# Turning one tile in eight of u with TensorE instead of VectorE's blocks, in a one-core spectral MoE kernel

## The chip, the core and the metric

The program runs on one core of one Trainium2 chip. The metric is the device time of one execution in microseconds. One execution of each program was also recorded by the hardware profiler; its span runs from the first to the last instruction of the program and is a little shorter than the device time. Engines are named as in the profile: PE (TensorE matmul), PEld (its weight loads), DVE (VectorE), ACT (ScalarE), POOL (GpSimd) and SP (SyncE, which issues most transfers here).

## What is computed

Three stages follow each other: a spectral mixing layer (Fourier transform along the sequence, complex matrix, soft threshold, inverse transform), a soft mixture of experts, and a SoLU layer with layer norm. The change lies in the last one:

```python
def _moe2_ref(x, w_in, w_out, g_ln):
    h = x @ w_in
    h_max = np.max(h, axis=-1, keepdims=True)
    e = np.exp(h - h_max)
    sm = e / (np.sum(e, axis=-1, keepdims=True) + 1e-09)
    solu = h * sm
    mu = np.mean(solu, axis=-1, keepdims=True)
    var = np.mean((solu - mu) ** 2, axis=-1, keepdims=True)
    ln = (solu - mu) / np.sqrt(var + 1e-06) * g_ln
    return (ln @ w_out).astype(np.float32)
```

Here x has 24576 rows of 256, w_in is 256 x 1024 and w_out 1024 x 256. All of it is wanted in fp32 precision.

## The kernel before, in words

`phase1` does the spectral layer and the sums of the mixture for eight batches. `phase2` does the experts, and then the SoLU layer in a loop over `NI` = 192 tiles of 128 rows. Only that loop changes, so only it is told here.

The mixture's output is never stored: it has rank 32 per batch, and `gst` holds the slots' outputs already multiplied by w_in, split into a high and a low part on the partitions, while `ctt` holds the combine weights. So `hmat(i)` makes h of tile i with two matmuls of 512 columns into `hps`, a PSUM tile of two banks from a pool of three. With the sign turned, `rowmax(i)` (DVE, line 996) reduces h, `expo(i)` (ACT, line 1003) takes the exponential and its row sum, and `umul(i)` (DVE, line 1011) forms u = h times e with its row sum. `vari(i)` (ACT, line 1087) sums the squares for the variance. The mean and g are folded into the weights `gw` beforehand, and the row's scale is applied when the result leaves PSUM.

For the last product u must be transposed, in eight blocks of 128 columns. `blocks(i)` has DVE transpose u in 32 x 32 squares (line 1027, tile `tb`) and then issues four transfers on SP (line 1031), which move the squares between partitions into `t2`. `tb` and `t2` have three buffers each. `uhi(i)` rounds t2 to fp32r, six blocks on ACT (line 1067) and two on POOL (line 1068), and `ulo(i, n)` forms the rest, t2 minus its rounded part, on POOL in two halves (line 1077). `prod(i)` is then 24 matmuls of 256 columns in fp32r: high part times high weights and times low weights (16), low part times high weights (8). Tiles come in pairs in one PSUM bank (`po2`, two buffers): the product of an even tile has to wait until both outputs of the pair four tiles earlier have been copied out by `outp` (ACT, line 1129). `rstd` makes the scales of four tiles at a time on POOL (lines 1112 to 1115). The last two tiles (`direct`) are turned by PE (`trans`, `direct_parts`) with `gstn`, a copy of `gst` in the natural order of columns, since `blocks` wants its columns permuted.

The order is written by hand: every engine runs its instructions in the order in which the loop at the end of `phase2` writes them. In turn i of the loop PE gets `hmat(i + 3)` and `prod(i - 3)`; DVE `rowmax(i + 2)`, `umul(i + 1)`, `blocks(i + 1)`; ACT `outp(i - 6)`, `vari(i)`, `expo(i + 2)`, `uhi(i - 1)`; POOL its share of `uhi(i - 1)`, `ulo(i - 1)` and `rstd(i)`. SP also gets the stores of the output (line 1140, every fourth turn) and the loads of `ct` (line 861, four transfers every eighth turn). In turns 24 to 30 `last_c` adds eight operations on POOL (lines 1153 and 1154), and in turn 40 `gst_order` adds one (line 1019). A tile of u has four buffers, `uh` and `ul` have four each.

Of the kernel before, what the change touches and what calls it, by code (L numbers as in the profile page):

```python
# [35 lines left out]
def kernel(  # L36
# [808 lines left out]
    def phase2(p2: ExitStack, pw: ExitStack):  # L845
# [3 lines left out]
        gw = k_p.tile([128, 8, 2, D], F32R, name="gw")  # L849
        gw_h, gw_l = gw[:, :, 0, :], gw[:, :, 1, :]  # L850
        gst = k_p.tile([128, DFF], F32R, name="gst")
        gstn = k_p.tile([128, DFF], F32R, name="gstn")
        cts = {}


# [96 lines left out]
        def right(name, bufs, **k):  # L952
            return p2.enter_context(tc.tile_pool(name=name, bufs=bufs, side="right", **k))

        e_p = right("e_p", 2)
        u_p = right("u_p", 4)
        o_p = right("o_p", 2)
# [19 lines left out]
        def hmat(i):  # L977
            if i >= NI:
                return
            j, k = divmod(i, 4)  # L980
            ps = ph_p.tile([128, DFF], F32, name="hps", tag="hps")
            for fh in range(2):
                mm(ps[:, 512 * fh:512 * fh + 512], ctt[j][:, 128 * k:128 * k + 128], (gstn if direct(i) else gst)[:, 512 * fh:512 * fh + 512])
            hps[i] = ps

        def stats(i):
# [19 lines left out]
        def umul(i):  # L1006
            if i >= NI:
                return
            st, k = stats(i)
            u = u_p.tile([128, DFF], F32, name="u", tag="u")  # L1010
            DVE.scalar_tensor_tensor(out=u, in0=hps.pop(i), scalar=1.0, in1=et.pop(i), op0=ALU.mult, op1=ALU.mult, accum_out=st[:, 2, k:k + 1])  # L1011
            ut[i] = u


        def direct(i):
            return i >= NI - 2

        def gst_order():
            POOL.tensor_copy(out=gstn.rearrange("p (c j b) -> p b c j", c=8, b=4), in_=gst.rearrange("p (b c j) -> p b c j", b=4, c=8).bitcast(F32))

        def blocks(i):
            if i >= NI or direct(i):
                return
            t = u_p.tile([128, DFF], F32, name="tb", tag="tb", bufs=3)
            DVE.transpose(out=t, in_=ut[i])  # L1027
            t2 = u_p.tile([128, 4, 256], F32, name="t2", tag="t2", bufs=3)
            for a in range(4):
                z = slice(32 * a, 32 * a + 32)  # L1030
                SP.dma_start(out=t2[:, a, :], in_=t[z].rearrange("i (b x) -> i b x", b=4))  # L1031
            t2t[i] = t2
# [23 lines left out]
                DVE.tensor_tensor(out=ul[:, z, :], in0=ps[:, z, :], in1=uh[:, z, :].bitcast(F32), op=ALU.subtract)  # L1056


        HA = 6

        def uhi(i):
            if i < 0 or direct(i):
                return
            uh, ul = parts(i)
            v = t2t[i].rearrange("p a (c j) -> p c a j", c=8)
            w = uh.rearrange("p c (a j) -> p c a j", a=4)
            ACT.activation(out=w[:, 0:HA], in_=v[:, 0:HA], func=AF.Copy)  # L1067
            POOL.tensor_copy(out=w[:, HA:8], in_=v[:, HA:8])  # L1068

        def ulo(i, n):  # L1070
            if i < 0 or direct(i):
                return
            uh, ul = uht[i]
            z = slice(4 * n, 4 * n + 4)
            v = t2t[i].rearrange("p a (c j) -> p c a j", c=8)[:, z]
            w = uh[:, z, :].rearrange("p c (a j) -> p c a j", a=4)
            POOL.tensor_tensor(out=ul[:, z, :].rearrange("p c (a j) -> p c a j", a=4), in0=v, in1=w.bitcast(F32), op=ALU.subtract)  # L1077
            if n:
                t2t.pop(i)
# [6 lines left out]
            sq = e_p.tile([128, DFF], F32, name="sq", tag="sq", bufs=1)  # L1086
            ACT.activation(out=sq, in_=ut.pop(i), func=AF.Square, bias=st[:, 2, k:k + 1], scale=-float(DFF), accum_out=st[:, 3, k:k + 1])  # L1087

        def prod(i):
            if i < 0 or i >= NI:  # L1090
                return
            uh, ul = uht.pop(i)
            if i % 2 == 0:
                pot[i // 2, 0] = po_p.tile([128, 2, D], F32, name="po2", tag="po2")
            ps = pot[i // 2, 0][:, i % 2, :]
            for f in range(8):
                mm(ps, uh[:, f, :], gw[:, f, 0, :], f == 0, False)
                mm(ps, uh[:, f, :], gw[:, f, 1, :], False, False)
            for f in range(8):
                mm(ps, ul[:, f, :], gw[:, f, 0, :], False, f == 7)  # L1100
            pot[i] = ps


        def rstd(i):
# [9 lines left out]
            POOL.tensor_tensor(out=st[:, 3, k], in0=st[:, 3, k], in1=st[:, 1, k], op=ALU.add)  # L1114
            POOL.tensor_tensor(out=st[:, 4, k], in0=st[:, 3, k], in1=mhalf[:, k], op=ALU.pow)

        o_todo = {}

        def outp(i):
            if i < 0:  # L1120
# [55 lines left out]
        blocks(0)  # L1176
        for i in range(NI + 6):
            j, k = divmod(i, 4)
            hmat(i + 3)
            trans(i)  # L1180
            rowmax(i + 2)
            umul(i + 1)
            blocks(i + 1)
            store(i - 6)
            late_c(i)
            last_c(i)
            outp(i - 6)
            vari(i)
            expo(i + 2)
            direct_parts(i)  # L1190
            if i <= NI:
                uhi(i - 1)
                ulo(i - 1, 0)
            rstd(i)
            if i <= NI:
                ulo(i - 1, 1)
            if i == 40:
                gst_order()
            if k == 1:
                pieces(j + 2)  # L1200
            prod(i - 3)
        while o_todo:
            store(min(o_todo))

# [139 lines left out]
```

## Time and profile before

| | us |
|---|---|
| device time, three runs | 1366.03, 1366.82 (median), 1371.24 |
| span of the profiled execution | 1364.4 |
| the loop over 192 tiles, first u (654.31) to the end of the span | 710 |
| DVE busy in the span | 1207.1 (88%) |
| PE busy in the span | 1268.9 (93%) |

The profiled execution's own device time is not listed apart; its span lies 2.4 us below the median of the runs and 1.6 us below the fastest, which is what lies around the first and the last instruction. A share of the whole span says little here, since the program has stages with different limits; the loop is read by itself. Starts within the span are read as they stand in the timeline, in us from the span's start.

### The profile page before, as it was taken

How to read it: one execution, taken by the hardware profiler on the slowest of the kernel's cores; microseconds unless marked ns; L12 is line 12 of the kernel's file. 1: busy time of each engine (PE TensorE's matmuls, PEld its weight loads, DVE VectorE, ACT ScalarE, POOL GpSimd, SP SyncE). 2: the span in 40 equal slices, each digit the busy share in tenths (PEclk: the TensorE clock that was granted, in tenths of full speed). 3: DMA queues.
4: the chain of work that ended last, by engine and by line, in shares of the span. 5: the costliest groups of instructions: out<-in, count | busy, mean ns of one | idle time of the engine just before them, and what ended most of it. 6: DMA issues, size and time to landing. Idle time of an engine off the chain costs nothing.

```text
span 1364.4 us, 30891 instructions
## 1 busy us (share of the span) xinstructions
PE 1268.9 (93%) x10784; PEld 1126.9 (83%) x10784; DVE 1207.1 (88%) x1691; ACT 1038.8 (76%) x2005; POOL 979.4 (72%) x1045
## 2 busy tenths in 40 slices
PE   6999999999999999878699989999999999899998
PEld 3888888888878788855588888988898889888897
DVE  7787988888888989765999999999999999999994
ACT  5567665666667665533799889999899999899995
POOL 5557575757565654221588989989899999889996
PEclk8899999999999999999799999999999999999999
DMA  8966463646445464168478788778877888787874
GB/s 267 289 202 175 124 193 111 209 117 186 140 144 167 126 181 155 62 223 291 108 179 220 188 210 209 198 197 209 205 194 203 196 198 217 196 206 191 201 197 125
DMA packets 190746, 252.70 MB, mean 185 GB/s; under 512 B 21504, under 2 KB 155392, under 8 KB 190592
## 3 DMA queue, kind: packets, MB, share of 16 engines
q1 hardware_dynamic: 190256, 249.57, 67.3%
q8 instruction: 85, 1.39, 0.4%
q10 hardware_dynamic: 336, 1.18, 0.2%
q14 instruction: 69, 0.57, 0.1%
HBM read 91.94 MB, written 59.11 MB: 111 GB/s over the span
## 4 chain that ended last, share of the span: by engine, by line
PE 37%; POOL 14%; DMA 13%; issue 12%; DVE 10%; SPq 8%; ACT 6%; POOLq 0%; ACTq 0%; DVEq 0%
PE po L89 10%; DMA t<-tb 9%; POOL ul L1077 8%; PE pb L89 6%; PE pm L89 6%; SPq L1031 6%; PE s L89 4%; PE xps L89 4%; PE pa L89 3%; DMA xc<-in_x_dram 3%; POOL x L235 2%; PE sps L92 2%; SPq L861 2%; POOL uh L1068 2%; ACT uh L1067 1%
## 5 line engine op out<-in xcount | busy, mean ns | idle before, releaser
L1077 POOL TENSOR_TENSOR ul<-t,uh 128x512 fp32r<-128x512 f32 x380 | 486.1, 1296 | 31.8 <-ACT uh L1067 30.7
L89 PEld LDWEIGHTS po<-gw,uh 128*128 128x128 f32 x3072 | 384.9, 190 | 80.8 <-ACT osb L1129 72.2
L89 PE MATMUL po<-gw,uh 128*128 128x256 f32 x3072 | 404.9, 284 | 41.7 <-ACT osb L1129 41.4
L346 POOL TENSOR_TENSOR s<-yb,s 128x512 f32<-128x512 f32 x95 | 132.4, 1394 | 216.9 <-DVE s L345 187.8
L1027 DVE STREAM_TRANSPOSE tb<-u 128x1024 f32<-128x1024 f32 x190 | 236.7, 1246 | 7.0 <-DMA t<-tb 0.4
L1011 DVE SCALAR_TENSOR_TENSOR u<-hps,e 128x1024 f32<-128x1024 f32 x192 | 232.3, 1210 | 11.6 <-ACT e L1003 11.1
L996 DVE TENSOR_REDUCE st<-hps 128x1 f32<-128x1024 f32 x192 | 227.7, 1186 | 1.7 <-PE hps L89 1.7
L1087 ACT ACTIVATE sq<-u,st 128x1024 f32<-128x1024 f32 x192 | 221.3, 1152 | 0.2 <-DVE u L1011 0.2
L1003 ACT ACTIVATE e<-hps,st 128x1024 f32<-128x1024 f32 x192 | 214.1, 1115 | 7.2 <-DVE st L996 6.6
L89 PE MATMUL po<-gw,ul 128*128 128x256 f32 x1536 | 213.0, 281 | 0.8 <-POOL ul L1077 0.8
L89 PEld LDWEIGHTS po<-gw,ul 128*128 128x128 f32 x1536 | 195.3, 189 | 1.1 <-POOL ul L1077 1.0
L1067 ACT ACTIVATE uh<-t 128x768 fp32r<-128x768 f32 x190 | 160.5, 845 | 44.6 <-DMA t<-tb 41.1
L235 POOL TENSOR_TENSOR x<-xc,x 96x512 fp32r<-96x512 f32 x120 | 164.7, 1381 | 29.5 <-ACT x L234 28.4
L89 PE MATMUL hps<-gst,ct 128*128 128x512 f32 x380 | 119.5, 397 | 12.0 <-DVE u L1011 10.5
L261 ACT ACTIVATE asb<-s 96x512 f32<-96x512 f32 x112 | 66.6, 595 | 73.8 <-PE s L89 73.2
L89 PE MATMUL s<-x,df_h 96*96 96x512 f32 x240 | 105.0, 440 | 12.9 <-ACT x L234 4.6
L1068 POOL CAST uh<-t 128x256 fp32r<-128x256 f32 x190 | 75.9, 400 | 49.9 <-DMA t<-tb 46.3
L89 PEld LDWEIGHTS xps<-d_sb,apt 128*128 128x128 f32 x768 | 99.4, 194 | 14.1 <-issue 2.9
L89 PE MATMUL xps<-d_sb,apt 128*128 128x128 f32 x768 | 105.8, 281 | 2.1 <-DMA apt<-ad 1.6
L1129 ACT ACTIVATE osb<-po,st 128x256 f32<-128x256 f32 x192 | 89.5, 468 | 10.2 <-PE po L89 9.1
L234 ACT ACTIVATE x<-xc 96x512 fp32r<-96x512 f32 x120 | 75.1, 626 | 13.2 <-DMA xc<-in_x_dram 13.2
L297 DVE TENSOR_TENSOR xsum<-xps,xi 128x256 f32<-128x256 f32 x96 | 39.8, 414 | 47.9 <-ACT xh L296 44.8
(204 smaller groups left out, 2232.1 us busy)
## 6 DMA issues: line engine op xcount, KB each, us to landing
t<-tb SPq DMA_DIRECT2D x760, 128.0 KB, 2.8
apt<-ad SPq DMA_DIRECT2D x96, 256.0 KB, 4.2
out_dram<-osb SPq DMA_DIRECT2D x47, 512.0 KB, 3.7
xc<-in_x_dram SPq DMA_DIRECT2D x56, 384.0 KB, 3.9
ad<-asb SPq DMA_DIRECT2D x56, 384.0 KB, 3.4
ct<-c_dram SPq DMA_DIRECT2D x96, 128.0 KB, 3.9
wt<-in_moe_w_dram SPq DMA_DIRECT2D x21, 512.0 KB, 8.8
ws<-in_moe_w_dram SPq DMA_DIRECT2D x22, 256.0 KB, 5.9
```

What stands on the lines that cost most here:

```text
L89: PE.matmul(out=out, lhsT=lhsT, rhs=rhs, start=start, stop=stop)
L235: POOL.tensor_tensor(out=lo, in0=t, in1=hi.bitcast(F32), op=ALU.subtract)
L346: (DVE if last else POOL).tensor_tensor(out=s, in0=y, in1=s, op=ALU.subtract)
L996: DVE.tensor_reduce(out=st[:, 0, k:k + 1], in_=hps[i], op=ALU.min, axis=AX.X)
L1003: ACT.activation(out=e, in_=hps[i], func=AF.Exp, bias=st[:, 0, k:k + 1], scale=-1.0, accum_out=st[:, 1, k:k + 1])
L1011: DVE.scalar_tensor_tensor(out=u, in0=hps.pop(i), scalar=1.0, in1=et.pop(i), op0=ALU.mult, op1=ALU.mult, accum_out=st[:, 2, k:k + 1])
L1027: DVE.transpose(out=t, in_=ut[i])
L1067: ACT.activation(out=w[:, 0:HA], in_=v[:, 0:HA], func=AF.Copy)
L1068: POOL.tensor_copy(out=w[:, HA:8], in_=v[:, HA:8])
L1077: POOL.tensor_tensor(out=ul[:, z, :].rearrange("p c (a j) -> p c a j", a=4), in0=v, in1=w.bitcast(F32), op=ALU.subtract)
L1087: ACT.activation(out=sq, in_=ut.pop(i), func=AF.Square, bias=st[:, 2, k:k + 1], scale=-float(DFF), accum_out=st[:, 3, k:k + 1])
L1129: ACT.activation(out=o[:, k], in_=pot.pop(i), func=AF.Copy, scale=stt[j][:, 4, k:k + 1])
```

## The change

For a tile i with i % 8 == 4 and 16 < i < 190, 22 tiles (20, 28, ... 188), `blocks(i)` is left out: no transpose on DVE and no transfers. Instead `turn(i)` at the head of turn i of the loop has PE transpose u in eight blocks of 128 x 128 back into the tile's own `hps`, and ACT copies all 1024 columns of it to SBUF in fp32 (`raw`, the buffer of `uh`). `hmat` of these tiles uses `gstn`. `prod(i)` then takes blocks 0 to 3 in native fp32 against `gwf`, the unsplit weights, and blocks 4 to 7 in fp32r as before (12 matmuls); for these POOL makes the rounded part and the rest (`turned_parts`, one cast and one subtraction of 512 columns). In turn i of a turned tile PE's order is `turn(i)`, the first 12 matmuls of `prod(i - 3)`, `hmat(i + 3)`, the rest of `prod(i - 3)`; and ACT does `expo(i + 2)` ahead of `vari(i)`. `gwf` is summed on POOL in turns 10, 12, 14 and 16 (`gw_sum`), and `gst_order` moves from turn 40 to turn 8. The pieces of the diff:

```diff
+        def turned(i):
+            return i % 8 == 4 and 16 < i < NI - 2
+
+        def gw_sum(n):
+            z = slice(2 * n, 2 * n + 2)
+            POOL.tensor_tensor(out=gwf[:, z], in0=gw[:, z, 0].bitcast(F32), in1=gw[:, z, 1].bitcast(F32), op=ALU.add)
+
         def blocks(i):
-            if i >= NI or direct(i):
+            if i >= NI or direct(i) or turned(i):
                 return
...
+        def turn(i):
+            ps = hps.pop(i).rearrange("p (c j) -> p c j", c=8)
+            for c in range(8):
+                tp(ps[:, c, :], ut[i][:, 128 * c:128 * c + 128])
+            raw, hl = parts(i)
+            ACT.activation(out=raw.bitcast(F32), in_=ps, func=AF.Copy)
+
+        def turned_parts(i, n):
+            raw, hl = uht[i]
+            r = raw[:, 4:8].bitcast(F32)
+            if n == 0:
+                POOL.tensor_copy(out=hl[:, 0:4], in_=r)
+            else:
+                POOL.tensor_tensor(out=hl[:, 4:8], in0=r, in1=hl[:, 0:4].bitcast(F32), op=ALU.subtract)
...
+                if turned(i):
+                    ops = [(uh[:, f, :].bitcast(F32), gwf[:, f, :]) for f in range(4)]
+                    hi = [(f, ul[:, f - 4, :], ul[:, f, :]) for f in range(4, 8)]
+                else:
+                    ops = []
+                    hi = [(f, uh[:, f, :], ul[:, f, :]) for f in range(8)]
+                for f, h, _ in hi:
+                    ops += [(h, gw[:, f, 0, :]), (h, gw[:, f, 1, :])]
+                ops += [(l, gw[:, f, 0, :]) for f, _, l in hi]
...
+            while len(ops) > (12 if part == 0 else 0):
+                mm(*ops.pop(0))
...
         for i in range(NI + 6):
             j, k = divmod(i, 4)
+            if turned(i):
+                turn(i)
+                prod(i - 3, 0)
             hmat(i + 3)
...
-            vari(i)
-            expo(i + 2)
+            if turned(i):
+                expo(i + 2)
+                vari(i)
+            else:
+                vari(i)
+                expo(i + 2)
...
-            if i == 40:
+            if i == 8:
                 gst_order()
+            if i in (10, 12, 14, 16):
+                gw_sum(i // 2 - 5)
...
-            prod(i - 3)
+            prod(i - 3, 1 if turned(i) else None)
```

PE's order around the first turned tile, i = 20. `po_9959` is the pair of tiles 16 and 17, `po_10066` (before: `po_10057`) that of tiles 18 and 19. Before:

```order
L89 MATMUL po_9957<-gw,uh 128x256 x16
L89 MATMUL po_9957<-gw,ul 128x256 x8
L89 MATMUL hps<-gst,ct 128x512 x2
L89 MATMUL po_9957<-gw,uh 128x256 x16
L89 MATMUL po_9957<-gw,ul 128x256 x8
L89 MATMUL hps<-gst,ct 128x512 x2
L89 MATMUL po_10057<-gw,uh 128x256 x16
L89 MATMUL po_10057<-gw,ul 128x256 x8
```

Now:

```order
L89 MATMUL po_9959<-gw,uh 128x256 x16
L89 MATMUL po_9959<-gw,ul 128x256 x8
L92 MATMUL hps<-ident,u 128x128 x8
L89 MATMUL po_9959<-gw,uh 128x256 x12
L89 MATMUL hps<-gst,ct 128x512 x2
L89 MATMUL po_9959<-gw,uh 128x256 x4
L89 MATMUL po_9959<-gw,ul 128x256 x8
L89 MATMUL hps<-gst,ct 128x512 x2
L89 MATMUL po_10066<-gw,uh 128x256 x16
L89 MATMUL po_10066<-gw,ul 128x256 x8
```

The eight transposes stand ahead of the product of tile 17, whose matmuls stand on both sides of `hmat(23)`; the next product that needs a new bank is that of tile 18, one `hmat` later.

ACT's order at the same place. The two `osb` rows of `po_9862` are the outputs of tiles 14 and 15, `sq` and `e` lines are `vari` and `expo`, and `uh<-hps` is the new copy:

```order
L1118 ACTIVATE sq,st<-u,st 128x1024
L1005 ACTIVATE e,st<-hps,st 128x1024
L1094 ACTIVATE uh<-t_9846 128x768
L1073 ACTIVATE uh<-hps 128x1024
L1169 ACTIVATE osb<-po_9862,st 128x256
L1005 ACTIVATE e,st<-hps,st 128x1024
L1118 ACTIVATE sq,st<-u,st 128x1024
L1094 ACTIVATE uh<-t_9896 128x768
L1169 ACTIVATE osb<-po_9862,st 128x256
L1118 ACTIVATE sq,st<-u,st 128x1024
L1005 ACTIVATE e,st<-hps,st 128x1024
L1169 ACTIVATE osb<-po_9959,st 128x256
```

The copy stands ahead of the output of tile 14, and the output of tile 15 follows it after four more operations; in the turn after, the rounding `uh<-t` is missing.

The semaphores that PE waits for in the same stretch, now:

```order
L92 MATMUL hps<-ident,u 128x128 [waits DVE_49]
L92 MATMUL hps<-ident,u 128x128 x7
L89 MATMUL po_9959<-gw,uh 128x256 x12
L89 MATMUL hps<-gst,ct 128x512 [waits DVE_49,PE_49]
L89 MATMUL hps<-gst,ct 128x512
...
L89 MATMUL hps<-gst,ct 128x512 [waits DMAHW6_49,DMAHW5_49,DMAHW7_49,DMAHW4_49,Activation_49]
L89 MATMUL hps<-gst,ct 128x512
L89 MATMUL po_10066<-gw,uh 128x256 [waits Activation_49]
L89 MATMUL po_10066<-gw,uh 128x256 x11
```

The transposes wait for DVE's u of tile 20; `hmat(23)` waits for DVE (u of tile 21, whose buffer it takes), `hmat(24)` for ACT's copy of tile 20, and the product of tile 18 for ACT's output of tile 15.

## Rows read from the trace of the kernel before

**Rows 1.** Busy time by stretch: loop's start, body, end; columns in the first row.
```profile
core 0: us, PE busy (x) PEld busy (x) DVE busy (x) ACT busy (x) POOL busy (x), PEclk, DMA share, GB/s
655.00:671.00 16.00, 7.79 (x28) 5.85 (x29) 15.83 (x20) 12.57 (x22) 6.50 (x8) 0.57 0.56 123
815.00:1333.00 518.00, 487.16 (x3745) 456.71 (x3744) 505.31 (x576) 483.94 (x865) 473.64 (x579) 1.00 0.81 201
1336.00:1351.00 15.00, 14.72 (x124) 14.42 (x123) 9.19 (x13) 13.42 (x26) 13.60 (x23) 1.00 0.53 147
```

**Rows 2.** Timeline of the body, PEld, DVE and ACT: start, duration, instruction, count.
```profile
1000.83 0.30 PEld L89 LDWEIGHTS hps<-gst,ct 128*128 128x128 f32 x2
...
1000.95 1.25 DVE L1027 STREAM_TRANSPOSE tb<-u 128x1024 f32<-128x1024 f32 x1
...
1002.12 1.19 DVE L996 TENSOR_REDUCE st<-hps 128x1 f32<-128x1024 f32 x1
...
1003.50 0.46 ACT L1129 ACTIVATE osb<-po,st 128x256 f32<-128x256 f32 x1
...
1003.86 1.14 ACT L1087 ACTIVATE sq<-u,st 128x1024 f32<-128x1024 f32 x1
...
1004.48 1.25 DVE L1027 STREAM_TRANSPOSE tb<-u 128x1024 f32<-128x1024 f32 x1
...
1004.99 1.11 ACT L1003 ACTIVATE e<-hps,st 128x1024 f32<-128x1024 f32 x1
...
1005.99 0.19 ACT L1003 ACTIVATION_READ_ACCUMULATOR e<-hps,st 128x1 f32 x1
1006.08 0.84 ACT L1067 ACTIVATE uh<-t 128x768 fp32r<-128x768 f32 x1
...
1006.82 0.46 ACT L1129 ACTIVATE osb<-po,st 128x256 f32<-128x256 f32 x1
...
1010.65 0.30 PEld L89 LDWEIGHTS hps<-gst,ct 128*128 128x128 f32 x2
```

**Rows 3.** Timeline, DVE: start, duration, instruction; u of tiles 20, 44 and 188.
```profile
725.03 1.21 DVE L1011 SCALAR_TENSOR_TENSOR u<-hps,e 128x1024 f32<-128x1024 f32 x1
814.74 1.21 DVE L1011 SCALAR_TENSOR_TENSOR u<-hps,e 128x1024 f32<-128x1024 f32 x1
1333.24 1.21 DVE L1011 SCALAR_TENSOR_TENSOR u<-hps,e 128x1024 f32<-128x1024 f32 x1
```

**Rows 4.** Who waited for whom in the loop: us in total, times, longest.
```profile
PEld po L89 <- ACT osb L1129: 71.7, 86, 2.7
...
ACT uh L1067 <- DMA t<-tb: 41.1, 40, 2.4
```

**Rows 5.** Timeline, POOL: what turns 24 and 40 add, and two ordinary subtractions.
```profile
747.80 0.40 POOL L1153 CAST cl_h<-cl 96x256 fp32r<-96x256 f32 x1
...
748.96 0.40 POOL L1068 CAST uh<-t 128x256 fp32r<-128x256 f32 x1
749.32 2.56 POOL L1077 TENSOR_TENSOR ul<-t,uh 128x512 fp32r<-128x512 f32 x2
...
811.98 2.06 POOL L1019 CAST gstn<-gst 128x1024 fp32r<-128x1024 f32 x1
```

**Rows 6.** Timeline at the loop's end: PE transposes u of a last tile.
```profile
1340.21 1.94 PEld L89 LDWEIGHTS po<-gw,uh 128*128 128x128 f32 x16 [0.48 <-ACT osb L1129]
...
1343.04 0.90 PEld L92 LDWEIGHTS pu<-ident,u 128*128 128x128 f32 x8
1343.14 1.03 PE L92 MATMUL pu<-ident,u 128*128 128x128 f32 x8
...
1343.90 1.97 PEld L89 LDWEIGHTS po<-gw,uh 128*128 128x128 f32 x16
```

**Rows 7.** Timeline of two overlapping windows in phase 1: native fp32, 256 columns, PE.
```profile
603.25 1.46 PE L89 MATMUL pgm<-wo,ones 128*128 128x256 f32 x6
603.68 1.03 PE L89 MATMUL pgm<-wo,ones 128*128 128x256 f32 x4
```

More of the change, by code (lines that the diff above doesn't have):

```diff
@@ L851, in phase2 @@
         gst = k_p.tile([128, DFF], F32R, name="gst")
-        gstn = k_p.tile([128, DFF], F32R, name="gstn")
         cts = {}
@@ L953, in right @@
             return p2.enter_context(tc.tile_pool(name=name, bufs=bufs, side="right", **k))
+        f_p = right("f_p", 1)
+        gwf = f_p.tile([128, 8, D], F32, name="gwf")
+        gstn = f_p.tile([128, DFF], F32R, name="gstn")
         e_p = right("e_p", 2)
@@ L982, in hmat @@
             for fh in range(2):
-                mm(ps[:, 512 * fh:512 * fh + 512], ctt[j][:, 128 * k:128 * k + 128], (gstn if direct(i) else gst)[:, 512 * fh:512 * fh + 512])
+                mm(ps[:, 512 * fh:512 * fh + 512], ctt[j][:, 128 * k:128 * k + 128], (gstn if direct(i) or turned(i) else gst)[:, 512 * fh:512 * fh + 512])
             hps[i] = ps
@@ L1010, in umul @@
             u = u_p.tile([128, DFF], F32, name="u", tag="u")
-            DVE.scalar_tensor_tensor(out=u, in0=hps.pop(i), scalar=1.0, in1=et.pop(i), op0=ALU.mult, op1=ALU.mult, accum_out=st[:, 2, k:k + 1])
+            DVE.scalar_tensor_tensor(out=u, in0=hps[i] if turned(i) else hps.pop(i), scalar=1.0, in1=et.pop(i), op0=ALU.mult, op1=ALU.mult, accum_out=st[:, 2, k:k + 1])
             ut[i] = u
@@ L1062, in uhi @@
             if i < 0 or direct(i):
+                return
+            if turned(i):
+                turned_parts(i, 0)
                 return
@@ L1071, in ulo @@
             if i < 0 or direct(i):
+                return
+            if turned(i):
+                if n:
+                    turned_parts(i, 1)
                 return
@@ L1087, in vari, with prod @@
             ACT.activation(out=sq, in_=ut.pop(i), func=AF.Square, bias=st[:, 2, k:k + 1], scale=-float(DFF), accum_out=st[:, 3, k:k + 1])
-        def prod(i):
+        def prod(i, part=None):
             if i < 0 or i >= NI:
                 return
[L1092 to L1101, printed above, removed]
+            if part != 1:
+                uh, ul = uht.pop(i)
+                if i % 2 == 0:
+                    pot[i // 2, 0] = po_p.tile([128, 2, D], F32, name="po2", tag="po2")
+                ps = pot[i // 2, 0][:, i % 2, :]
+                if turned(i):
[7 more added lines that the diff above has]
+                ops += [(l, gw[:, f, 0, :]) for f, _, l in hi]
+                pot[i] = ps
+                pr_ops[i] = [(ps, a, b, n == 0, n == len(ops) - 1) for n, (a, b) in enumerate(ops)]
+            ops = pr_ops[i]
+            while len(ops) > (12 if part == 0 else 0):
+                mm(*ops.pop(0))
         def rstd(i):
@@ L1115, in rstd @@
             POOL.tensor_tensor(out=st[:, 4, k], in0=st[:, 3, k], in1=mhalf[:, k], op=ALU.pow)
-        o_todo = {}
+        o_todo, pr_ops = {}, {}
         def outp(i):
@@ L1178, in phase2 @@
             j, k = divmod(i, 4)
+            if turned(i):
+                turn(i)
+                prod(i - 3, 0)
             hmat(i + 3)
@@ L1187, in phase2 @@
             outp(i - 6)
-            vari(i)
-            expo(i + 2)
+            if turned(i):
+                expo(i + 2)
[3 more added lines that the diff above has]
+                expo(i + 2)
             direct_parts(i)
```

## The prediction

> **What bounds the kernel now.** I read the busy time by stretch first, then the timeline of a few tiles, then the list of waits, then the order that the change makes. In the body of the loop no engine is much ahead: over 518 us DVE is busy 505.3, PE 487.2, ACT 483.9 and POOL 473.6 us, with the clock of PE at its upper level of 2.4 GHz, granted 1.00 [rows 1]. So the question is not who is busiest but in what steps each of them moves. In the timeline [rows 2] the reader is to subtract starts, since the durations overlap by about 0.1 us. DVE goes from one transpose to the next in 1004.48 - 1000.95 = 3.53 us, ACT from one output to the next in 1006.82 - 1003.50 = 3.32 us, and PE through three tiles in 1010.65 - 1000.83 = 9.82, so 3.27 us each. DVE is the slowest. Eight tiles of it are 8 x 3.53 = 28.24 us. What is measured is a little more: from u of tile 44 to that of tile 188 there are 18 groups of eight, (1333.24 - 814.74) / 18 = 28.81 us each, and from tile 20 to tile 44 three groups of (814.74 - 725.03) / 3 = 29.90 us [rows 3]. The rest over 28.24 is waiting: ACT waits 41.1 us in 40 places for moved squares of u, and so comes late with the exponential that DVE needs. PE waits 71.7 us, almost all of it at the start of an even tile's product for ACT's outputs [rows 4]; that PE waits while it is nearly full is what matters below.
>
> **What goes, per turned tile.** DVE saves one transpose, 1002.12 - 1000.95 = 1.17 us [rows 2], so its eight tiles fall to 27.07. SP loses four issues and the ring of three t2 buffers skips a tile, which can only relieve ACT's waits for them. POOL loses one cast of 256 columns and one of its two subtractions and gains a cast of 512: the subtraction is 1.28 (two in 2.56) and the cast 0.40 [rows 5], taken twice for 512 columns, so about 0.9 us less. It is not the bound.
>
> **What comes on PE.** Eight transposes take 1343.90 - 1343.04 = 0.86 us from weight load to weight load [rows 6]. The Trainium skill, TensorE: Matmul & The Clock Gate, Part 4, gives about 275 ns for one PE transpose in a kernel's context; if they followed each other at that, eight would be 2.2 us and the sum below 1.3 us per group higher, an estimate from that page. The row is eight of them in a stream in this loop, so the sum goes by it.
>
> Of the product, four blocks go native. Two views of the same fp32 matmuls of 256 columns start 0.43 us apart with two instructions fewer, so one takes 0.215, and a native product is two of them, 0.43 us [rows 7]. An fp32r block is three matmuls; 24 of them take 1343.04 - 1340.21 = 2.83 us after a wait [rows 6], so 0.118 each and 0.354 a block. Four blocks cost 4 x (0.43 - 0.354) = 0.30 us more. The Trainium skill, FP8 and Floating Point Precision, TensorE Precision Notes, says that true fp32 makes four passes; four at 0.118 would be 0.47 and add 0.47 instead of 0.30 us. I keep the measured row. PE's eight tiles become 8 x 3.27 + 0.86 + 0.30 = 27.3 us, now above DVE's 27.07.
>
> **What comes on ACT.** A copy of 1024 columns from PSUM is not in the trace in this form. The exponential reads the same 1024 PSUM columns and releases the engine after 1005.99 - 1004.99 = 1.00 us, with a duration of 1.11 [rows 2]; I take 1.00 and keep 0.90 and 1.11 as bounds. It replaces a rounding of 0.74 (1006.08 to 1006.82). ACT's eight tiles become 8 x 3.32 + 0.26 = 26.8 us.
>
> By shares alone the group would fall from 28.81 to about 27.3. **But the change adds a loop through two engines.** The copy waits for PE's transposes. Behind it on ACT, in order, stand the output of tile i - 6, the exponential, the squares, a rounding and the output of tile i - 5; and PE's product of tile i - 2, an even tile, waits for that last output, as the order and the semaphores show. From PE's first transpose to that product:
>
> - transposes, first load to last end: 1343.14 + 1.03 - 1343.04 = 1.13 [rows 6]
> - copy 1.00; output 1003.86 - 1003.50 = 0.36; exponential 1006.08 - 1004.99 = 1.09; squares 1004.99 - 1003.86 = 1.13; rounding 0.74; last output 0.46 [rows 2], and 0.05 that I allow for the signal (a choice, without a row).
>
> That is 5.96 us. PE itself has in the meantime 0.86 of transposes, 2.83 of the product of tile i - 3, and two `hmat` of 3.27 - 2.83 = 0.44: 4.57 us. So it stands still for 1.39 us. `hmat(i + 3)` in between waits for u of tile i + 1 and not for the copy, and DVE has that ready 2.4 us after u of tile i, where PE arrives after 0.86 + 12 x 0.118 = 2.3 us; I cost it at nothing, since DVE, with 1.7 us to spare in a group, is ahead by then, and at 0.1 without that cover. From the product of tile i - 2 to the next transposes PE has seven products and six `hmat`: 7 x 2.83 + 6 x 0.44 + 0.30 = 22.75 us. The loop closes in 5.96 + 22.75 = **28.71 us**, against 28.81 now. DVE's 1.17 us are bought back by PE's stop: PE is the bound in place of DVE, and DVE (27.07), ACT (26.8) and POOL have 1.6 us or more to spare in each group, enough to swallow their small waits.
>
> **The first tiles.** POOL gets `gst_order` in turn 8 (2.06 us) and four sums in turns 10 to 16 (1.28 each, as the subtractions [rows 5]): 7.2 us in nine turns, on an engine that is 91% busy [rows 1]. What such a load costs is seen in tiles 20 to 44: `last_c` adds four times 748.96 - 747.80 = 1.16 us and turn 40 adds 2.06, 6.7 us in all [rows 5], and the three groups take 3 x (29.90 - 28.24) = 5.0 us more than DVE needs [rows 3]. So 0.75 us per us. Bounds for the early load: 0, if POOL's backlog stays behind the buffers, and 7.2; 0.75 of it would be 5.4. I take 4, since the start has no backlog yet. In the three groups, with turn 40's part gone, 4.64 x 0.75 = 3.5 us stand over 28.24; 1.4 of this vanishes under the new floor (3 x 0.47), so they take 86.1 + 2.1 = 88.2 instead of 89.7 us: -1.5.
>
> **The sum.** 18 x (28.71 - 28.81) = -1.8, first tiles +4, the three groups -1.5: +0.7 us. The profiled span of 1364.4 becomes 1365.1; the runs' median lies 2.4 above that span, and so I give **1367.5 us**, no change that a measurement could tell (about 0.5%, 6.8 us). Bounds: the copy at 0.90 and a signal of nothing give 28.56 a group, -3.2 over 21 groups; without the early cost -4; so 1360. A group at 29.1, if a wait for moved squares now and then falls into the loop, gives +8, and the early load at its full price +3: 1379.
>
> **Rivals.**
> *DVE's saving comes through.* If PE's stop were covered, PE's 27.3 us would be the group: 18 x 1.5 + 3 x 2.6 - 4 = 31 us less, 1336. For it: PE waits 71.7 us for outputs now and is still not the bound [rows 4], so such waits can be free. Against it: they are free because DVE sets the pace, and in the new order nothing stands between copy and outputs that could be skipped. Half of it would need the chain of 5.96 to be 0.7 shorter than its rows. Chance 0.14 for anything over 0.5% faster.
>
> *The loop catches ACT's transfers* (the slower side). The rounding inside the chain reads what four transfers have moved of tile i - 1; a wait for them now lengthens a path with no slack. Today one in five roundings waits, 41.1 / 40 = 1.03 us [rows 4]. If each turned tile met one, +1.03 x 21 = 22 us: 1389; it decides from about one in three (+7 us). Against it: SP has four issues less just before. Chance 0.2.
>
> *The clock falls.* In 655 to 671, where PE had long pauses, the granted clock was 0.57, mostly the lower level of 1.2 GHz [rows 1]. If the transposes with the stop behind them did this, the 4.6 us of PE's work in the turned turn would double: at most 4.6 x 22 = 100 us, and half of that, 1418, if it falls in every second. Against it: 1336 to 1351 holds sixteen transposes between products at 1.00 [rows 1]. The Trainium skill, TensorE: Matmul & The Clock Gate, Part 4, says that transposes don't count as busy for the clock; that last stretch does not bear it out. Chance 0.03.
>
> *The change isn't what it says*, as if fewer tiles were turned: the order shows eight transposes for 22 tiles, so 0.01; it would give the time of before.
>
> **How the numbers follow.** Forecast (a group at 28.5 to 29.1) 0.62 with the last rival's 0.01 in it; faster 0.14; slower 0.2 + 0.03, and 0.01 for an early POOL load that costs more than its full price. Chances: 0.14, 0.62, 0.24. The range 1360 to 1379 leaves out most of the first rival, and the second only where nearly every tile is hit.
>
> **What would show it.** Right: u of tiles 44 to 188 stay 28.5 to 29.1 us per eight; DVE's busy share of the body falls from 98% to some 94%; PE waits for `osb` about 1.4 us at the product after each set of transposes and hardly elsewhere; the copy starts 1.1 us after the first transpose. Wrong: groups under 28.2 (the chain is shorter than I read it, or the stop is hidden), groups over 29.3 with waits of `uh` for transfers right after the copy, or a granted clock under 1.00 in the body. A stall over 5 us before tile 20 would say that the early POOL load was priced too low.

## The result, and the profile after

| | before | after |
|---|---|---|
| device time, median of four runs (lowest to highest), us | 1368.69 (1366.03 to 1371.24) | 1386.43 (1384.64 to 1388.71) |
| span of the profiled execution, us | 1364.4 | 1385.6 |
| first u to u of tile 20 | 70.72 | 70.70 |
| u of tile 20 to u of tile 44, three groups of eight | 89.71 | 91.74 |
| u of tile 44 to u of tile 188, eighteen groups | 518.50 | 538.22 |
| one of these eighteen | 28.81 | 29.90 |

The change made the kernel slower: the ratio is 1.0135, with a 95% interval of 1.0114 to 1.0156. The forecast was 1367.5 us, with a range that ended at 1379. The table says where the time went. Of 21.2 us of span, 19.7 lie in the body of the loop and 2.0 in the three groups before it; the two ends of the program give back 0.5. In the body sixteen of the eighteen groups take 29.2 to 30.4 us after, one takes 32.75 (last section) and one 28.8. The early load on POOL, which ends before tile 20, costs nothing.

The u of tiles 20, 44 and 188 on DVE in the profile after, which answer to [rows 3] (start, duration, instruction):

```profile
723.30 1.21 DVE L1013 SCALAR_TENSOR_TENSOR u<-hps,e 128x1024 f32<-128x1024 f32 x1
815.04 1.21 DVE L1013 SCALAR_TENSOR_TENSOR u<-hps,e 128x1024 f32<-128x1024 f32 x1
1353.26 1.21 DVE L1013 SCALAR_TENSOR_TENSOR u<-hps,e 128x1024 f32<-128x1024 f32 x1
```

The busy time of the body after, with the columns of [rows 1]:

```profile
815.00:1353.00 538.00, 505.61 (x3817) 477.76 (x3816) 486.87 (x559) 487.17 (x866) 454.44 (x559) 1.00 0.71 175
```

DVE did lose its transposes: it is busy 486.9 us of 538, or 90%, where it had 98% before. But no engine took its place as the full one; PE has 94%, as before. The group became longer while every engine has idle time, so the body is set by a chain of waits that runs through several engines. The clock of PE is 1.00.

The waits of the body, after (us in total, times, longest):

```profile
PEld po L89 <- ACT osb L1169: 47.4, 35, 2.5
...
ACT uh L1094 <- DMA t<-tb: 29.2, 19, 3.1
DVE u L1013 <- ACT e L1005: 24.0, 35, 2.3
DVE st L998 <- PE hps L89: 22.8, 18, 2.7
```

The same view of the kernel before, for its body:

```profile
PEld po L89 <- ACT osb L1129: 54.0, 69, 2.7
ACT uh L1067 <- DMA t<-tb: 32.1, 29, 2.4
...
DVE u L1011 <- ACT e L1003: 6.9, 13, 0.9
...
DVE st L996 <- PE hps L89: 0.4, 1, 0.4
```

Here the reader sees what became of DVE's saving. DVE waited for the exponential and for h 7.3 us in the body before (6.9 and 0.4); now it waits 46.8, 2.2 us more in each group, nearly twice what it saved (1.17). ACT's waits for moved squares hardly changed (32.1 and 29.2). PE waits less often for outputs, but for nearly as long: 35 times in eighteen groups, so about two stops in each.

### The first stop is the forecast's

The timeline of PE's weight loads around a turned tile, tile 100, after (an idle time and what ended it stand in brackets):

```profile
1030.49 0.90 PEld L92 LDWEIGHTS hps<-ident,u 128*128 128x128 f32 x8
1031.36 1.49 PEld L89 LDWEIGHTS po<-gw,uh 128*128 128x128 f32 x12
1032.78 0.31 PEld L89 LDWEIGHTS hps<-gst,ct 128*128 128x128 f32 x2
...
1036.47 1.94 PEld L89 LDWEIGHTS po<-gw,uh 128*128 128x128 f32 x16 [1.52 <-ACT osb L1169]
...
1042.90 1.71 PEld L89 LDWEIGHTS po<-gwf,uh 128*128 128x128 f32 x8
1044.64 1.59 PEld L89 LDWEIGHTS po<-gw,ul 128*128 128x128 f32 x12
```

and ACT in the same stretch:

```profile
1031.72 1.03 ACT L1073 ACTIVATE uh<-hps 128x1024 f32<-128x1024 f32 x1 [1.17 <-issue]
1032.64 0.47 ACT L1169 ACTIVATE osb<-po,st 128x256 f32<-128x256 f32 x1
...
1034.08 1.15 ACT L1118 ACTIVATE sq<-u,st 128x1024 f32<-128x1024 f32 x1
...
1035.22 0.84 ACT L1094 ACTIVATE uh<-t 128x768 fp32r<-128x768 f32 x1
1035.95 0.47 ACT L1169 ACTIVATE osb<-po,st 128x256 f32<-128x256 f32 x1
```

From the first transpose to the product of tile 98 it is 1036.47 - 1030.49 = 5.98 us, in the order that was forecast, and the mean over the eighteen groups is 5.98 too. PE stands still for 1.52 us. The rounding inside this chain waits for nothing.

### The second stop is not

Twenty microseconds later, in the same group, PE waits again, at the product of tile 104, for the output of tile 101. PE's weight loads:

```profile
1057.40 1.96 PEld L89 LDWEIGHTS po<-gw,uh 128*128 128x128 f32 x16 [1.07 <-ACT osb L1169]
1060.25 0.90 PEld L92 LDWEIGHTS hps<-ident,u 128*128 128x128 f32 x8
```

ACT, ahead of that output:

```profile
1056.14 0.85 ACT L1094 ACTIVATE uh<-t 128x768 fp32r<-128x768 f32 x1 [1.62 <-DMA t<-tb]
1056.90 0.45 ACT L1169 ACTIVATE osb<-po,st 128x256 f32<-128x256 f32 x1
```

And SP's queue of transfers before that:

```profile
1037.34 10.17 SPq L1040 DMA_DIRECT2D t<-tb  x12
1047.55 0.60 SPq L1180 DMA_DIRECT2D out_dram<-osb  x1
1048.26 2.45 SPq L860 DMA_DIRECT2D ct<-c_dram  x4
1050.87 7.24 SPq L1040 DMA_DIRECT2D t<-tb  x11
```

ACT waits 1.62 us for the moved squares of tile 105. SP issued these moves from 1050.87, since an output store (0.60) and the four loads of `ct` (2.45) stood ahead of them: 3.3 us from 1047.55. DVE had the squares ready well before that:

```profile
1047.02 1.25 DVE L1036 STREAM_TRANSPOSE tb<-u 128x1024 f32<-128x1024 f32 x1
```

That is 2.6 us from the end of the transpose (1048.26) to the first issue. The last of the four moves then landed 3.2 us after its issue, where that of tile 101 took 2.7, so most of the delay is the place in SP's queue and not the transfer itself. The loads of `ct` come every eighth turn, so this meets the same tile of every group: in the body after, ACT waits before the rounding of the tile with i % 8 = 1 in 17 groups of 18, 1.47 us on average over all eighteen, 26.5 us in all.

The kernel before has the same wait at the same place, as its ACT and its SP show:

```profile
1045.81 0.84 ACT L1067 ACTIVATE uh<-t 128x768 fp32r<-128x768 f32 x1 [2.00 <-DMA t<-tb]
```

```profile
1037.26 0.60 SPq L1140 DMA_DIRECT2D out_dram<-osb  x1
1037.97 2.42 SPq L861 DMA_DIRECT2D ct<-c_dram  x4
1040.54 11.23 SPq L1031 DMA_DIRECT2D t<-tb  x16
```

There it comes in 17 of 18 groups too, 1.34 us on average, 24.1 us of the body's 32.1. It cost little, because DVE set the pace and lost only 0.3 to 0.4 us of it in a group.

### The profile page after: what moved, and what is told of

Same layout as the page of the kernel before. It is cut to its first block, busy times and chain, and to the rows that moved or that the text cites. A ratio compares the mean times of both kernels' runs of the same rounds, so it can differ in the third digit from the quotient of the medians.

```text
span 1385.6 us, 30699 instructions
## 1 busy us (share of the span) xinstructions
PE 1289.1 (93%) x10872; PEld 1151.9 (83%) x10872; DVE 1179.9 (85%) x1669; ACT 1042.5 (75%) x2005; POOL 962.6 (69%) x1027
## 3 DMA queue, kind: packets, MB, share of 16 engines
q10 hardware_dynamic: 336, 1.18, 0.2%
## 4 chain that ended last, share of the span: by engine, by line
PE 40%; DMA 12%; SPq 10%; issue 10%; POOL 10%; ACT 9%; DVE 8%; ACTq 0%; POOLq 0%; DVEq 0%
PE po L89 9%; DMA t<-tb 8%; SPq L1040 7%; PE pb L89 7%; PE pm L89 6%; POOL ul L1108 6%; PE s L89 5%; PE xps L89 4%; PE pa L89 3%; ACT e L1005 2%; SPq L860 2%; PE sps L92 2%; ACT sq L1118 2%; ACT uh L1094 2%; POOL x L235 2%
## 5 line engine op out<-in xcount | busy, mean ns | idle before, releaser
L1108 POOL TENSOR_TENSOR ul<-t,uh 128x512 fp32r<-128x512 f32 x336 | 428.8, 1292 | 65.0 <-ACT uh L1094 63.9
L89 PEld LDWEIGHTS po<-gw,uh 128*128 128x128 f32 x2720 | 345.0, 190 | 72.7 <-ACT osb L1169 62.7
L89 PE MATMUL po<-gw,uh 128*128 128x256 f32 x2720 | 361.7, 284 | 43.1 <-ACT osb L1169 42.7
L89 PE MATMUL po<-gw,ul 128*128 128x256 f32 x1624 | 228.2, 284 | 0.3 <-POOL ul L1108 0.3
L1036 DVE STREAM_TRANSPOSE tb<-u 128x1024 f32<-128x1024 f32 x168 | 209.3, 1246 | 5.8
L89 PEld LDWEIGHTS po<-gw,ul 128*128 128x128 f32 x1624 | 207.8, 189 | 1.8 <-POOL ul L1108 0.5
L1094 ACT ACTIVATE uh<-t 128x768 fp32r<-128x768 f32 x168 | 144.4, 860 | 37.5 <-DMA t<-tb 36.9
L89 PE MATMUL hps<-gst,ct 128*128 128x512 f32 x336 | 106.5, 400 | 11.5 <-DVE u L1013 10.1
L1095 POOL CAST uh<-t 128x256 fp32r<-128x256 f32 x168 | 67.0, 399 | 53.9 <-DMA t<-tb 50.7
L1169 ACT ACTIVATE osb<-po,st 128x256 f32<-128x256 f32 x192 | 92.7, 484 | 10.4 <-PE po L89 7.8
L297 DVE TENSOR_TENSOR xsum<-xps,xi 128x256 f32<-128x256 f32 x96 | 39.8, 414 | 50.5 <-ACT xh L296 47.4
```

Of the source, the lines that this page charges most:

```text
L1169: ACT.activation(out=o[:, k], in_=pot.pop(i), func=AF.Copy, scale=stt[j][:, 4, k:k + 1])
```

## The experiments

Two theories stood against each other. **S** (two stops): the chain behind the turned tile is as forecast, and what it lacked is the wait for tile i + 5, which now reaches PE at a place where PE, stopped once in each group already, has nothing left to give. **A** (the chain alone): the order of ACT behind the copy costs the time, and with the two outputs ahead of the copy it would come back. Further rivals came with single runs: **P** (PE's own work is the bound), **L** (the early sums on POOL delay the first turned tiles) and **N** (they cost nothing), **D** (DVE's saving is still at work, so DVE's transposes, put back, would add their time). Each kernel ran beside the kernel before; ratios are to that one.

| | ACT's chain long | two outputs first |
|---|---|---|
| `ct` loads ahead of the moves of tile i + 5 | 29.90 (after) | 29.69 (e2) |
| `ct` loads in a turn without moves | 28.99 (e1) | 27.98 (e3) |

This table has the main result ahead of the single runs: the us of one group of eight tiles, mean of eighteen in the traced execution. The 29.69 of e2 is on the high side, as is told there.

### e1: the loads of ct in the turn that has no moves

A turned tile issues no moves, so in the turn that would have held them SP is free. The loads are put there, half a period later.

```diff
-                c_todo[4 * j + 3] = (b + 1, h)
+                c_todo[4 * j + 7] = (b + 1, h)
```

> The changed kernel with one edit: the four loads of ct on SP move from turn 7 of each eight to turn 3 of the next eight, the turn in which SP has no moves of a turned tile to issue. Theory S (a second stop of PE: ACT waits some 1.5 us for the moved squares of tile i + 5, which stand on SP behind the store and the four loads, its output comes late and PE waits for it at the product of tile i + 4): the wait before that rounding falls under 0.4 us, PE's stop there goes, a group of eight tiles falls from 29.90 to 28.7 to 28.9 us and the run to 1358 to 1368 us. Theory P (PE simply has too much work, the native products or the transposes cost more than the rows gave): the group stays at 29.6 us or more, 1380 to 1388.

Measured: 1371.63 us (1369.04 to 1376.00, ten runs), ratio 1.0026 (1.0012 to 1.0039). Its waits in the body, and its u of tiles 44 and 188:

```profile
PEld po L89 <- ACT osb L1169: 30.5, 23, 1.5
...
ACT uh L1094 <- DMA t<-tb: 6.5, 7, 1.7
```

```profile
817.29 1.21 DVE L1013 SCALAR_TENSOR_TENSOR u<-hps,e 128x1024 f32<-128x1024 f32 x1
1339.15 1.21 DVE L1013 SCALAR_TENSOR_TENSOR u<-hps,e 128x1024 f32<-128x1024 f32 x1
```

ACT's waits fall from 29.2 to 6.5 us, PE's second stop is gone (30.5 us in 23 places is little more than eighteen first stops), and the group is (1339.15 - 817.29) / 18 = 28.99 us, where the forecast had 28.71. The first chain is still 5.98. So one line of the schedule gives back most of the loss, and it changes no engine's work. Group and time came a little above what S gave (28.9 and 1368); tiles 20 to 44 took 91.55 us, as many as after.

### e2: the two outputs ahead of the copy

ACT gives out the outputs of tiles i - 6 and i - 5 before it copies the turned tile, which shortens the first chain and leaves the loads where they were.

```diff
+                outp(i - 6)
+                outp(i - 5)
                 turn(i)
...
-            outp(i - 6)
+            if not (turned(i) or turned(i - 1)):
+                outp(i - 6)
```

> The changed kernel with one edit: in a turned tile's turn ACT does the outputs of tiles i - 6 and i - 5 ahead of the copy, so that PE's product of tile i - 2 no longer waits for the chain behind the copy. Theory S (both stops of PE exist, but the loop that sets the pace runs from the transposes over h of tile i + 3, DVE, SP's queue, ACT and the product of tile i + 4): the way from the transposes to the product of tile i - 2 falls from 5.98 to 4.6 us, yet the group only to 29.4 to 29.9 us, the run 1375 to 1387. Theory A (the chain behind the copy alone sets the pace): the group falls by the whole 1.4 us to 28.5, the run to about 1357.

Measured: 1379.20 us (1377.60 to 1386.52, five runs), ratio 1.0076 (1.0055 to 1.0096). The chain from the first transpose to the product of tile i - 2 falls from 5.98 to 4.5 us, as meant, and the group only from 29.90 to 29.69. The waits of the body:

```profile
PEld po L89 <- ACT osb L1169: 34.7, 18, 3.4
...
ACT uh L1094 <- DMA t<-tb: 31.7, 19, 3.4
```

One stop in each group is left, and it is the second one, longer than before: 2.0 us on average (1.34 to 3.42) in place of 1.18. So it takes back 0.8 of the 1.5 us that the first gave up. The traced execution took 1386.52 us, 7.3 over the median of the five runs, so the group's usual length is under 29.69: some 29.3, an estimate that puts all of these 7.3 us into the eighteen groups. Part of the 29.69 is a clock effect, told at the end. Theory A falls by the median too, which is 22 us above the 1357 that it gave: the chain alone is not what costs the time.

### e3: both edits

The two diffs above together.

> The changed kernel with both edits: the loads of ct in the free turn of SP, and the outputs of tiles i - 6 and i - 5 ahead of the copy. Theory S: with both stops gone PE's own work (27.3 us) and DVE's (27.1) are the bound, the group comes to 27.4 to 28.2 us and the run to 1332 to 1350. Theory P: no lower than 29 us a group, 1366 or more. Theory A: the same as with the outputs alone.

Measured: **1352.33 us** (1351.10 to 1354.33, four runs), ratio 0.9883 (0.9865 to 0.9900). It is faster than both kernels. Its waits in the body, and its u of tiles 44 and 188:

```profile
DVE st L998 <- PE hps L89: 12.8, 18, 1.2
PEld po L89 <- ACT osb L1169: 9.8, 13, 1.6
ACT uh L1094 <- DMA t<-tb: 8.3, 9, 1.6
```

```profile
815.44 1.21 DVE L1013 SCALAR_TENSOR_TENSOR u<-hps,e 128x1024 f32<-128x1024 f32 x1
1319.03 1.21 DVE L1013 SCALAR_TENSOR_TENSOR u<-hps,e 128x1024 f32<-128x1024 f32 x1
```

With neither stop the group is (1319.03 - 815.44) / 18 = 27.98 us, 0.83 under the kernel before. Each edit alone gave 0.91 and 0.21 of a group, both together 1.92; by the ratios of the whole runs to the kernel before it is 1.1% and 0.6% alone and 2.5% together. So the two stops are on one loop: in e2 the second grew when the first went. The time is a little above the upper end of what was expected, again by tiles 20 to 44 (91.6 us).

In six of the eighteen groups, of 27.48 to 27.57 us from one set of transposes to the next, PE doesn't stop once, so 27.5 is PE's own work. The others are longer by what is left of the second stop, 9.3 us in all. The record shows where it is left: ACT waits 0.86 to 1.58 us before the rounding of tiles 73, 97, 121, 145 and 169, 24 tiles apart, 0.73 at tile 185, and at most 0.18 at the other twelve. Before just these five roundings (0.5 to 4.5 us ahead) the trace has a DMA packet of 16 KB on a queue that the page of the profile lists as an instruction queue (packets, MB, share):

```profile
q8 instruction: 86, 1.41, 0.4%
```

In e3's body, moves land 3.62 us after their issue on average when such a packet starts in the first 2.5 us (73 moves), else 2.82 (433), and the same holds in all twelve traces (3.45 to 3.67 against 2.80 to 2.84). This is a coincidence in time, seen everywhere; no run moves these packets, so that they cause the wait is not shown.

### e4 and e9: less work on PE

In e4, blocks 0 to 3 of a turned tile get one fp32r matmul each in place of the native product, and ACT's copy rounds to fp32r. In e9 the same is done to e3.

```diff
-            ACT.activation(out=raw.bitcast(F32), in_=ps, func=AF.Copy)
+            ACT.activation(out=raw, in_=ps, func=AF.Copy)
...
-                    ops = [(uh[:, f, :].bitcast(F32), gwf[:, f, :]) for f in range(4)]
+                    ops = [(uh[:, f, :], gw[:, f, 0, :]) for f in range(4)]
```

> The changed kernel with less work on PE: the four native fp32 products of a turned tile become one fp32r matmul each (rounded u against the high weights alone, so the low parts of half of these tiles' products are left out). PE has about 1.25 us less to do per turned tile. Theory S: the product of a turned tile is not on the loop that sets the pace, so the group stays at 29.5 to 29.9 us, 1378 to 1387. Theory P: the group falls by what PE saves, to about 28.7, 1361.

> The kernel with both edits and with less work on PE: the four native fp32 products of a turned tile become one fp32r matmul each (rounded u against the high weights alone, the low parts of half of these products left out), 1.25 us less for PE per turned tile. If PE's own work is the bound there now (27.3 us by rows), a group falls to DVE's 27.1 to 27.5 us and the run to 1335 to 1346; if DVE or the waits are, nothing changes, 1349 to 1355. Without both edits the same cut changed nothing (30.07 against 29.90).

Measured: e4 1392.56 us (two runs), ratio 1.0175 (1.0150 to 1.0201), group 30.07; e9 1353.06 us (two runs), ratio 0.9877 (0.9853 to 0.9902), group 28.01. PE has less to do in both and neither is faster. PE's waits for outputs in the body of e4, and then of e9:

```profile
PEld po L89 <- ACT osb L1169: 74.1, 54, 3.6
```

```profile
PEld po L89 <- ACT osb L1169: 36.6, 36, 1.6
```

PE waits 26.7 us longer than after in the one (74.1 against 47.4), and 26.8 longer than in e3 in the other: what was cut from its work (4 x 0.435 - 4 x 0.118, some 1.27 us a group, 22.8 in all, an estimate) it waits instead. Theory P falls for the kernel after. For e3 it falls only in part: PE is full in its groups of 27.5 us, but less work on PE gains nothing, since in e9 PE stops for some 1.2 us in each group at another product, that of the tile with i % 8 = 6, and the shortest group is 27.33. So other engines need nearly as long there.

### e10: DVE's transposes kept

The kernel after, with DVE's transpose of the turned tiles put back. Nobody reads it, and its moves stay away.

```diff
-            if i >= NI or direct(i) or turned(i):
+            if i >= NI or direct(i):
                 return
...
+            if turned(i):
+                return
```

> The changed kernel, with DVE's transpose of the turned tiles kept (into a block tile that nobody reads, no transfers), so that what the change saves on DVE is given back: 1.17 us per turned tile. Theory S (DVE stands still for more than that in the turned turn, 0.96 us before u of tile i + 1 and 1.26 before the maximum of tile i + 3): the group stays at 29.7 to 30.2 us, the run 1383 to 1391. Theory D (DVE still sets the pace): the group grows by 1.17, the run to about 1410.

Measured: 1388.81 us (1382.72 to 1390.12, four runs), ratio 1.0130 (1.0102 to 1.0157), the same as after; group 29.69. DVE's waits:

```profile
DVE st L998 <- PE hps L89: 13.4, 17, 1.2
...
DVE u L1013 <- ACT e L1005: 7.9, 21, 0.6
```

They fall from 46.8 to 21.3 us, by 25.5, as DVE's added work (18 x 1.17 = 21.1 us) goes into its idle time. Theory D falls: in the kernel after, what the change takes off DVE is worth nothing.

### e7: the kernel before, with the loads of ct spread

If the wait for the tile behind the loads is as old as this, it must be there to take away in the kernel before. The four loads are issued one in each of four turns.

```diff
-            if i in c_todo:
-                load_c(*c_todo.pop(i))
+            for n in range(4):
+                if i - n in c_todo:
...
+                        SP.dma_start(out=c_new[0][32 * n:32 * n + 32].rearrange("s a j -> s (a j)").bitcast(F32), in_=c_dram[b, n % 2, h])
```

> The kernel before with one edit: the four loads of ct go out one in each of turns 7, 8, 9 and 10 instead of all in turn 7. Theory S (the wait of ACT behind these loads is there before too, 1.34 us in nearly every group, and DVE loses some 0.4 us of it): the wait before the rounding of tiles 1 of 8 falls under 0.8 us, the group from 28.81 to 28.3 to 28.5 us, the run to 1358 to 1364. Against S (the wait has another cause, as the store of the output or POOL): wait and time stay, 1365 to 1370.

Measured: 1364.83 us (1362.93 to 1370.38, ten runs), ratio 0.9978 (0.9961 to 0.9996), group 28.62. ACT's waits in the body:

```profile
ACT uh L1067 <- DMA t<-tb: 21.2, 27, 1.7
```

The wait at the tile behind the loads falls from 1.34 to 0.77 us on average (it is still met in 17 of 18 groups), all waits from 32.1 to 21.2, and the group by 0.19. The time just misses the window that was expected. The group, too, is above the 28.3 to 28.5 that was expected. So the loads are a cause of that wait before the change too, and there it is worth only some 0.2%: 11 us of waits less make 3.4 us of time in the body.

### e5 and e6: the sums on POOL ahead of the loop

`gst_order` and the four `gw_sum` are made before the loop starts; in e5 in e3, in e6 in the kernel after.

```diff
+        for n in range(4):
+            gw_sum(n)
+        gst_order()
...
-            if i == 8:
-                gst_order()
-            if i in (10, 12, 14, 16):
-                gw_sum(i // 2 - 5)
```

> The kernel with both edits (loads of ct in the free turn, outputs ahead of the copy), and the four sums and the reordered gst done on POOL before the loop, where it idles for 38 us, in place of turns 8 to 16. Theory L (the early POOL load cost nothing before tile 20 only because it made PE later, from some 2.3 to 4.65 us behind u, and that lag is paid at the first turned tile): PE's first transposes start under 3 us after u of tile 20, tiles 20 to 28 take under 30.5 instead of 33.3 us, the run comes to 1347 to 1351. Theory N (the load is free; what is lost at tile 20 belongs to the first turned tile itself or to the later POOL work of turns 24 to 30): nothing changes, 1350 to 1354.

> The changed kernel with the sums and the reordered gst before the loop as its only edit. Theory L: tiles 20 to 28 take under 30 us instead of 31.7, the groups from tile 44 stay at 29.5 to 30.2, the run 1380 to 1385. Theory N: 1384 to 1389, tiles 20 to 28 as they were.

Measured: e5 1351.20 us (1349.41 to 1352.78, four runs), ratio 0.9872 (0.9849 to 0.9894); e6 1389.96 us (1386.07 to 1390.44, four runs), ratio 1.0153 (1.0130 to 1.0176). Neither differs from its kernel without the edit by more than the runs scatter. For the kernel after, theory L falls and N stands: tiles 20 to 28 take 31.7 us after and 32.1 in e6, and the early load on POOL is free. In e6, PE comes late to tile 20 because ACT has waited 2.48 us for the moves of tile 17, which again stand behind loads of `ct`. For e3 it is not settled. Tiles 20 to 28 take 33.3 us in e3 and 29.3 in e5, which is L's sign, and tiles 20 to 44 take 3.7 us less. But in the traced execution of e5 the first u comes 5.3 us later than in e3 (658.42 against 653.12), 5.2 us of it from stages ahead of the edit, and the time of 1351.20 lies in N's window and only 0.2 over L's.

### e8: one output store less ahead of the moves

e3 with every second store of the output put four turns later, and a third buffer for the output tile, to see whether the store is the rest of the wait. As it was written, two stores fell on the same turn and one took the place of the other, so this kernel leaves out every second store of the output.

```diff
-        o_p = right("o_p", 2)
+        o_p = right("o_p", 3)
...
-                o_todo[i + 2] = (v, o)
+                o_todo[i + 2 + 4 * (j % 2 and 3 < j < NG - 3)] = (v, o)
```

> The kernel with both edits, and every second store of the output issued four turns later, in the turn in which SP has no moves to issue (with a third buffer for the output tile). Theory S, carried on (what is left over 27.5 us in every second or third group is still ACT waiting behind the store on SP, mean 0.36 us before the rounding of tiles 1 of 8): that wait falls under 0.15 us, the group from 27.98 to 27.5 to 27.8, the run to 1342 to 1350. Against it: the rest has another cause, 1350 to 1355.

Measured: 1350.92 us (1346.62 to 1353.45, four runs), ratio 0.9868 (0.9848 to 0.9888), which e3's interval overlaps; group 27.88, and ACT's wait at the tile with i % 8 = 1 is 0.38 us, 0.36 in e3. Even with stores missing the wait doesn't shrink, so the store is not what is left over 27.5 us. The waits that are left stand at tiles 73, 97, 121, 145 and 169 again (0.75 to 1.39 us), and 0.80 at tile 185.

## Why the prediction was wrong

**What held.** The bound before was read rightly, and so was the chain: 5.96 us forecast, 5.98 measured, with a stop of 1.39 forecast and 1.52 seen. Its terms err a little against each other: the copy holds ACT for 1032.64 - 1031.72 = 0.92 us, not 1.00, but it starts 1031.72 - 1030.49 = 1.23 us after the first transpose, not 1.13. The rest of PE's round, forecast at 22.75, is 22.84 and 22.91 in the last two groups of the body after, where the second stop is away or small (0.23). PE's own work, forecast at 27.3, is 27.5 in e3. In e1, where the second stop is mostly away, the whole group is 28.99 us against 28.71.

PE's transposes take 1031.36 - 1030.49 = 0.87 us for eight, and the four native blocks 1044.64 - 1042.90 = 1.74, or 0.435 each (0.43 forecast). The Trainium skill's 275 ns for one transpose, which it gives for bf16 (TensorE: Matmul & The Clock Gate, Part 4), would by estimate have made eight 2.2 us; in this stream they follow each other at less than half of that. The Trainium skill's four passes for true fp32 (FP8 and Floating Point Precision, TensorE Precision Notes) would by estimate have made the four blocks 1.9 us; the trace has 1.74.

**The step that failed** is the sentence that ends the costing: DVE, ACT and POOL "have 1.6 us or more to spare in each group, enough to swallow their small waits". ACT's waits are not small and not spread. The total of 41.1 us in 40 places [rows 4] was read as one rounding in five, 1.03 us each, when most of it (24.1 of 32.1 us in the body before) stands at one tile of each eight. There it is 1.47 us after, and spare time later in the group cannot give it back, because the output behind that wait is what PE's next even product needs. PE had 28.71 us of work and of first stop in a group of 28.71, so it could not swallow it either. The account closes: PE's weight loads wait 47.4 us for outputs in the body, of which eighteen first stops at 1.52 are 27.4; the other 20.0 are seventeen second stops. Behind one of them sixteen matmuls take 1.4 us longer, at a lower clock (last section). Together that is 21.4 us, and 18 x (29.90 - 28.71) is 21.4. Two smaller terms cancel: PE's round without a second stop, 5.98 + 22.84, is 0.11 us a group over the forecast (2.0 in all), and the sixteen matmuls behind a second stop take 1.94 to 1.96 us instead of 2.06 to 2.08, which gives as much back.

The loop that sets the pace now is longer than the one forecast: transposes of tile i, h of tile i + 3, DVE's maximum of it (which waits 1.26 us on average), DVE's following turns, the moves of tile i + 5 behind the store and the loads of `ct`, ACT's rounding of it, the output of tile i + 1, the product of tile i + 4, and from there PE's queue to the transposes of tile i + 8. e1 takes the loads out of this loop, e2 takes the first stop out, and only e3 gets under the time of before.

**The rivals.** "The loop catches ACT's transfers" gave 1389, and 1386.43 was measured. But it had the wait at the rounding of tile i - 1, inside the short chain, and that rounding never waits in the body; the price was near for a reason that is not the one given. What spoke against it, "SP has four issues less just before", is true of that tile and doesn't bear on the other. "DVE's saving comes through" is what e3 comes near to: with both stops away the group is 27.98, against the 27.3 that this rival took. "The clock falls" did not happen at the transposes; the stretch 1336 to 1351 that was set against it has under 2 us of transposes in 15, so it was a weak argument. The change did what it says.

**The first tiles.** The early POOL load was put at +4 us and is 0, as the table at the top and e6 show; the price of 0.75 us per us, read from tiles 20 to 44, did not hold for this load. What those tiles lose is not shown. The three groups from tile 20 were forecast 1.5 us shorter and became 2.0 longer; PE has second stops of 0.52 and 1.99 us in them, at the products of tiles 24 and 32, of the same kind as in the body.

## What to carry to other kernels

Before a total of waits is spread evenly over its places, sort them by their position in the period of the program: a wait that comes at the same tile of every round is a term of the chain, with its full size, and what stands ahead of it in the transfer queue is the first suspect. When a change moves the bound from one engine to a loop through several, old waits can count again: ACT's wait behind the loads cost DVE 0.3 to 0.4 us a group before, and PE 1.1 after. And look at what the change frees: here the turn without moves was the place for the loads that made the other turns late.

## What was not expected of the hardware

A stop of PE can cost more than its length. In one group after, PE waited 2.53 us for an output, and the sixteen matmuls behind it took 3.37 us instead of 1.94. The weight load, and the busy time of that stretch with the columns of [rows 1]:

```profile
936.60 3.37 PEld L89 LDWEIGHTS po<-gw,uh 128*128 128x128 f32 x16 [2.53 <-ACT osb L1169]
```

```profile
934.00:936.60 2.60, 0.49 (x3) 0.07 (x1) 2.46 (x4) 1.26 (x3) 0.73 (x2) 1.00 0.78 186
936.60:940.00 3.40, 3.40 (x16) 3.40 (x17) 1.20 (x2) 2.90 (x5) 2.94 (x4) 0.52 0.88 265
```

The granted clock is 0.52 there, mostly the lower level of 1.2 GHz, behind a stretch in which PE was busy 0.49 of 2.60 us, and the eight transposes that follow take their usual 0.89 us. That group took 32.75 us, the longest of the body. The stop itself follows the longest of ACT's waits, 3.09 us at tile 73, one of the tiles told at e3. In e2, whose one stop is longer, it happened behind four stops of 2.46 to 3.42 us in the body, and in part behind one of 2.20, and the clock of its whole body is 0.98. The sixteen took 2.33 to 3.45 us there, 5.9 us more than at 1.94 in all, so some 0.3 us of its 29.69 a group comes from this; in e4 three such places (2.53, 2.89 and 3.27 us for the sixteen) cost 2.9 us, 1.4 more than the one after, which is about half of the 0.17 a group by which e4 is longer. It does not follow each long stop: in e4 one of 3.59 us was followed by sixteen in 1.96. So a stop can weigh more than its own microseconds, but how much more can't be read from its length.
